# Block-sparse attention with a gated convolution: all transfers planned as one stream, four query/key pairs turned on TensorE instead of six, and the third batch's convolution done on both query parts at once

## The chip, the cores and the metric

The kernel runs on one core of one Trainium2 chip. The metric is device time in microseconds (us) of one execution. Each execution carries a state, fast or slow, and comparisons below use fast runs unless a sentence says otherwise. A ratio is the mean time of one kernel's fast runs over the mean of the other kernel's fast runs of the same rounds, so it is not quite the ratio of the medians quoted beside it; the brackets are its 95% interval.

Names: PE is TensorE (matmuls), PEld its weight loads, DVE VectorE, ACT ScalarE, POOL GpSimd, SP SyncE. A suffix q ("SPq") is an engine's instruction queue, where transfers are issued.

## The reference

Four batches, eight heads, 768 tokens, 64 columns a head. The attention mask keeps the window, the first and last blocks and three random blocks of each row of blocks. The attention output goes into a feed-forward layer with a three-tap convolution along the sequence and a sigmoid gate.

```python
scores = scale * np.matmul(q, k.transpose(0, 1, 3, 2))
scores = np.where(mask, scores, -1000000000.0)       # mask: per block of 32 x 32
attn = np.exp(scores - max); attn /= attn.sum(-1)    # shortened
x = (attn @ v) as (batch, seq, 512)                  # shortened
h = np.maximum(x @ w_in, 0.0)                        # 512 -> 1024
conv_out[s] = sum over k of conv_w[k] * h[s + k - 1] # shortened
out = (h * sigmoid(conv_out)) @ w_out                # 1024 -> 512
```

## The kernel before

The program is planned before it is built. Every piece of work is an operation with a duration per engine, dependences and buffers. A list scheduler places the operations one after the other in a model of the engines, some passes back and forth, and what comes out is a fixed order of instructions for each engine. On the chip each engine keeps its order; an instruction whose input is not there holds up everything behind it (below, VectorE stands 7.41 us before a copy, and the copy behind it, whose own input was there, starts only after it). The durations and latencies of the model therefore change the order and hardly the work (a few operations, relus and output copies, may go to VectorE or ScalarE, as the planner finds). The two latencies of DMA transposes:

```python
XLAT, TLAT = 3.908, 9.2201     # comment added here: XLAT for attention results, TLAT for a pair's q and k, in us
```

The heads are worked on in 16 pairs. A pair's q and k must be transposed into the tiles `et` and `ot` of one of the slots. The first `NPE` pairs are turned by TensorE and evicted from PSUM; the rest go through a DMA transpose into `tmp`, and VectorE copies `tmp` to the slot:

```python
NSLOT = 6
NPE = 6
...
t0 = op({"SP": 1.3}, xp(0), due - 8, [lq], alloc=tb, uses=[nb], lat=TLAT)     # transpose of q
t1 = op({"SP": 1.3}, xp(1), due - 8, [lk], uses=[nb, tb], lat=TLAT)           # transpose of k
ce = op({"DVE": 0.5}, put(ET, 0), due, [t0, t1, slot_first.get(P - 1)], alloc=slot_b[P], uses=[tb])
co = op({"DVE": 0.5}, put(OT, 64), due, [ce], uses=[slot_b[P], tb])
```

A batch has two query parts of 384 tokens, each with 18 exponentials of 128x1024, 144 in all. The convolution works on 2 x 384 columns at a time (three multiplies, two additions, a tanh, "+1", a product with h):

```python
m1 = op({"DVE": tm}, mul(1, 0), due + 1.7, list(relus) + [cw_op], alloc=cb, uses=[heb])
m0 = op({"DVE": tm}, mul(0, 1), due + 2, [edge[0]], uses=[cb, heb])
ad1 = op({"DVE": t_d2(768)}, add, due + 2.2, [m1, m0], uses=[cb])
...
th = op({"ACT": 0.745}, ...Tanh...)
```

The mask is 24 extra rows of `et` and `ot`, the same in every slot. They are built once in slot 0 and copied; from slot 2 on SyncE copies them by DMA (`rows_to`), for slot 1 VectorE and GpSimd do.

The softmax here doesn't subtract the row's maximum and nothing guards it: scores larger than these inputs give would overflow.

## Time and profile before

| | before |
|---|---|
| median of the runs | 215.1 us (214.3 to 215.75) |
| profiled span | 214.9 us |
| first exponential starts / last ends | 8.2 / 184.5 us |
| VectorE busy / idle | 189.7 / 25.2 us |
| copies of `tmp` to a slot | pairs 6 to 15; VectorE never waits for one |

In this kernel VectorE's copies of a DMA-transposed tile find it there every time: among its waits there is none for `tmp`. The view of the tile `tmp` (line, engine, operation, count, duration ns min/median/max, first and last start; then the time from issue to landing):

```profile
L581 SPq DMA_TRANSPOSE tmp<-nat x20: 1211/1365/2948, 38.8 to 128.1; - x20
L424 DVE COPY et<-tmp x10: 542/544/741, 57.4 to 145.0; 64x1536 bf16<-64x1536 bf16 x10
DMA to landing us min/median/max: 6.0/6.5/6.9
```

The transposes begin at 38.8 us. The trace has the landing of only four of the twenty; these took 6.0 to 6.9 us, under the allowance of 9.2. The engines' busy lines and the stages are shown in the prediction below. Because busy and idle of VectorE add up to the span, I use those two numbers for every kernel later: a change in work shows in the first, a change in waiting in the second.

### The profile page before, as it was taken

Reading aid. Unit: us, or ns where it says so; the run is one execution under the profiler, and the core shown is the slowest. Engines: PE = TensorE matmul, PEld = TensorE weight load, DVE = VectorE, ACT = ScalarE, POOL = GpSimd, SP = SyncE. Lnnn points to the kernel's source line nnn. Section 1 sums busy time; section 2 is a strip of 40 time slices with the busy share of each in tenths; the row PEclk is TensorE's granted clock in tenths of the full one; section 3 lists DMA queues with packets and bytes.
Section 4 is the critical chain, followed back from the end, with each engine's and each line's share of the span. In section 5 each row is a group of like instructions: output and inputs, shape, how many; then the busy total and the mean of one; then the engine's idle time right before and its main releaser. Section 6 shows DMA issues by size and latency. Waiting matters only on the chain.

```text
span 214.9 us, 6588 instructions
## 1 busy us (share of the span) xinstructions
PE 198.8 (92%) x2579; PEld 150.4 (70%) x2596; DVE 189.7 (88%) x541; ACT 182.1 (85%) x227; POOL 81.8 (38%) x174
## 2 busy tenths in 40 slices
PE   7996999997999979999989999989999999998992
PEld 4785878886677857788768667667786787554441
DVE  6865627999989999479999999999999999999972
ACT  4595999999989989999998799989999999674541
POOL 8993414625505540446375302431241012443300
PEclk9999999999999999999999999999999999999999
DMA  6999994999999997899996993001110230022223
GB/s 170 152 177 204 199 203 61 142 154 134 190 136 212 150 119 80 148 146 213 168 136 106 129 204 107 18 20 62 59 23 21 71 116 21 18 98 101 99 98 146
DMA packets 50520, 25.84 MB, mean 120 GB/s; under 512 B 36321, under 2 KB 47353, under 8 KB 50489
## 3 DMA queue, kind: packets, MB, share of 16 engines
q0 software_dynamic: 18464, 11.14, 43.7%
q1 hardware_dynamic: 31592, 13.75, 31.6%
q10 hardware_dynamic: 432, 0.52, 0.7%
q8 instruction: 20, 0.33, 0.6%
q14 instruction: 12, 0.09, 0.2%
HBM read 23.08 MB, written 6.29 MB: 137 GB/s over the span
## 4 chain that ended last, share of the span: by engine, by line
DVE 59%; PE 15%; DMA 10%; ACT 6%; issue 5%; POOL 2%; SPq 1%; ACTq 0%; DVEq 0%; POOLq 0%
DVE m L753 19%; DVE m L759 10%; DVE hE L742 7%; PE st L678 6%; ACT pt L685 5%; DVE gT L781 5%; DVE xtok L631 5%; DMA nat<-in_k_dram 4%; DMA tmp<-nat 4%; PE mix L799 4%; DVE tn L772 3%; PE av L705 2%; DMA o2s<-in_q_dram 2%; DVE o2s L424 2%; PE st L799 2%
## 5 line engine op out<-in xcount | busy, mean ns | idle before, releaser
L685 ACT ACTIVATE pt<-st 128x1024 bf16<-128x1024 f32 x144 | 141.8, 1039 | 8.5 <-PE st L678 7.2
L705 PE MATMUL av<-vt,pt 128*128 128x65 bf16 x1152 | 57.9, 193 | 1.9 <-DVE vt L519 1.4
L753 DVE TENSOR_SCALAR m<-hE,cw 128x384 bf16<-128x384 bf16 x192 | 56.9, 346 | 0.2
L705 PEld LDWEIGHTS <-pt 128*128 128x128 bf16 x1152 | 50.4, 97 | 6.2 <-issue 1.7
L729 PE MATMUL mix<-xT,winb 128*128 128x384 bf16 x240 | 48.1, 325 | 1.9 <-DVE hE L742 1.1
L829 POOL COPY hE<-hE 128x254 bf16<-128x254 bf16 x32 | 18.4, 575 | 74.7 <-DVE hE L742 51.0
L799 PE MATMUL mix<-woutb,gT 128*128 128x512 bf16 x151 | 41.0, 379 | 2.4 <-DVE gT L781 1.6
L678 PE MATMUL st<-ot 88*128 88x128 bf16 (+1 forms) x224 | 42.5, 234 | 0.5 <-ACT pt L685 0.2
L678 PE MATMUL st<-et,ot 88*128 88x128 bf16 (+1 forms) x224 | 42.5, 234 | 0.1
L678 PE MATMUL st<-et 88*128 88x128 bf16 (+1 forms) x208 | 40.7, 239 | 1.7 <-ACT pt L685 1.7
L678 PEld LDWEIGHTS <-ot 88*128 88x128 bf16 x448 | 34.5, 97 | 10.1 <-issue 0.9
L678 PE MATMUL st<-ot,et 88*128 88x128 bf16 (+1 forms) x208 | 40.7, 239 | 0.7 <-ACT pt L685 0.4
L678 PEld LDWEIGHTS <-et 88*128 88x128 bf16 x416 | 32.3, 97 | 9.9 <-issue 3.3
L759 DVE TENSOR_TENSOR m<-m 128x768 bf16<-128x768 bf16 x64 | 35.1, 554 | 0.1
L769 ACT ACTIVATE tn<-m 128x768 bf16<-128x768 bf16 x32 | 27.7, 866 | 5.5 <-DVE m L759 5.4
L729 PEld LDWEIGHTS <-winb 128*128 128x128 bf16 x256 | 22.1, 97 | 13.1 <-issue 2.7
L799 PEld LDWEIGHTS <-gT 128*128 128x128 bf16 x200 | 16.5, 98 | 15.5 <-DVE gT L781 3.1
L742 DVE TENSOR_SCALAR hE<-mix 128x384 bf16<-128x384 f32 x37 | 20.2, 548 | 3.9 <-PE mix L729 3.8
L781 DVE TENSOR_TENSOR gT<-tn,hE 128x768 bf16<-128x768 bf16 x32 | 17.9, 562 | 0.1
L631 DVE TENSOR_TENSOR xtok<-av,rcp 128x384 bf16<-128x384 f32 x32 | 17.6, 549 | 0.3
L492 POOL DMA_DIRECT2D vn<-in_v_dram x16 | 11.9, 743 | 10.4 <-DVE vt L519 8.7
L830 POOL COPY hE<-hE 128x254 bf16<-128x254 bf16 x32 | 15.3, 479 | 0.0
(76 smaller groups left out, 168.7 us busy)
## 6 DMA issues: line engine op xcount, KB each, us to landing
out_dram<-o2s SPq DMA_DIRECT2D x23, 256.0 KB, 2.2
vn<-in_v_dram POOLq DMA_DIRECT2D x16, 192.0 KB, 6.2
nat<-in_q_dram POOLq DMA_DIRECT2D x15, 192.0 KB, 7.3
nat<-in_k_dram POOLq DMA_DIRECT2D x15, 192.0 KB, 6.4
winb<-in_moe_w_in_dram POOLq DMA_DIRECT2D x2, 512.0 KB, 12.2
woutb<-in_moe_w_out_dram POOLq DMA_DIRECT2D x2, 512.0 KB, 9.5
xT<-xtok SPq DMA_TRANSPOSE x27, 8.8
o2s<-in_k_dram ACTq DMA_DIRECT2D x2, 192.0 KB
```

What stands on the lines that cost most here:

```text
L631: nm = op({"DVE": 0.475}, lambda e: nc.vector.tensor_tensor(out=xtok_t[xk.index].rearrange("p c h d -> p h c d"), in0=o_of()[:, :, :, 0:64 ...
L678: nc.tensor.matmul(out=st_t[stb.index][:, 128 * x:128 * (x + n_)], lhsT=QK[kc % 2][s][0:88, 1, hh, kc // 2, :], rhs=QK[par][s][0:88, 0, hh ...
L685: e_op = op({"ACT": t_act(1024)}, lambda e, stb=stb, ptb=ptb: nc.scalar.activation(out=pt_t[ptb.index], in_=st_t[stb.index], func=AF.Exp, ...
L705: nc.tensor.matmul(out=av_t[av_buf[(n, P % 4)].index][:, off:off + 65], lhsT=pt_t[ptb.index][:, 128 * x:128 * x + 128], rhs=VT[P % NSLOT][ ...
L729: nc.tensor.matmul(out=tiles[hb.index][:, 0:384], lhsT=winb[:, fc, 128 * ffc:128 * ffc + 128], rhs=xT_t[xt_buf[n].index][:, fc, :], start= ...
L742: nc.vector.tensor_scalar(out=dst, in0=src, scalar1=0.5, scalar2=0.0, op0=ALU.mult, op1=ALU.max)
L753: nc.vector.tensor_scalar(out=m_t[cb.index][:, slot, o0:o1], in0=src, scalar1=w, scalar2=None, op0=ALU.mult)
L759: nc.vector.tensor_tensor(out=m[:, 0], in0=m[:, 0], in1=m[:, 1], op=ALU.add)
L769: th = op({"ACT": 0.745}, lambda e: nc.scalar.activation(out=tn_t[cb.index], in_=m_t[cb.index][:, 0], func=AF.Tanh, bias=0.0, scale=0.5), ...
L781: nc.vector.tensor_tensor(out=o, in0=t, in1=h, op=ALU.mult)
L799: nc.tensor.matmul(out=acc()[:, 0:o1 - o0], lhsT=gT_t[gb.index][:, ffc, 128 * c:128 * c + 128], rhs=woutb[:, ffc, o0:o1], start=(ffc == 0) ...
L829: nc.gpsimd.tensor_copy(out=h[:, f0:f0 + 2, 1:128], in_=h[:, f0:f0 + 2, 384:511])
```

## The change

The intent is to lighten all three compute engines and the early stream of loads at once: the planner models all transfers as one stream and issues loads a fixed time ahead; mask rows are copied by VectorE instead of DMA; two pairs fewer use TensorE and PSUM; the third batch's convolution works on both query parts in one instruction.

```diff
-FLEX = 0.0345
+FLEX = 0
+PATIENCE = {"PE": 0.1, "ACT": 0, "DVE": 0.05}
...
-                    k = (s, o.prio, o.key)
+                    k = (max(s, t + PATIENCE.get(e, 0.0)), o.prio, o.key)
...
-    NSLOT = 6
-    NPE = 6
+    NSLOT = 5
+    WIDE = (2,)
+    AHEAD = 11.181113366977723
+    NPE = 4
...
-    NTMP, NVN, NNAT, NPT, NXK, NXT, NHE, NCV, NGT, NOS = 2, 3, 3, 5, 3, 4, 3, 3, 4, 4
+    NTMP, NVN, NNAT, NPT, NXK, NXT, NHE, NCV, NGT, NOS = 2, 3, 3, 5, 3, 4, 2, 2, 2, 4
-    m_t = many(NCV, [128, 2, 768], BF16, "m")
-    tn_t = many(NCV, [128, 768], BF16, "tn")
+    m_t = many(NCV, [128, 2, 1536], BF16, "m")
...
-    XLAT, TLAT = 3.908, 9.2201
+    XLAT, TLAT = 1.0, 1.1986797974651535
...
+    def sp_dma(fn, sp, dur, prio, deps, lat, alloc=None, uses=(), by="SP"):
+        i_ = op({by: sp}, fn, prio, deps, lat=0.1, alloc=alloc, uses=uses)
+        return op({"DQ": dur}, None, prio, [i_], lat=lat, uses=list(uses) + ([alloc] if alloc else []))
...
-                m[s] = op({"SP": 0.46}, rows_to(t[s], t[0]), T(4.5 * s) - 6, [m[0]], lat=6.0, ...
+                m[s] = op({"DVE": 0.58}, rows_by(t[s], t[0]), T(4.5 * s) - 2.5, [m[0]])
...
-            t0 = op({"SP": 1.3}, xp(0), due - 8, [lq], alloc=tb, uses=[nb], lat=TLAT)
+            t0 = sp_dma(xp(0), 1.25, 1.1, due - 8, [lq], TLAT, alloc=tb, uses=[nb])
...
-        ad1 = op({"DVE": t_d2(768)}, add, due + 2.2, [m1, m0], uses=[cb])
+        ad1 = op({"DVE": t_d2(w)}, add, due + 2.2, [m1, m0], uses=[cb])      # w = 1536 in the wide batch
```

Cut: the new layout of `hE` and `gT` with both query parts in one tile, the edge columns, the tail, and the other knobs of the plan.

## The prediction

The 0.13, 0.07 and 0.11 us saved for each instruction that goes were estimates; what the traces show of them stands below the text.

> **What bounds the kernel now.** I read the page first (busy shares, the 40 slices, the chain), then a table of busy time by stage, then ScalarE's, VectorE's and SyncE's instructions in order of time, and last the groups with their shapes.
>
> ```profile
> PE 198.8 (92%) x2579; PEld 150.4 (70%) x2596; DVE 189.7 (88%) x541; ACT 182.1 (85%) x227; POOL 81.8 (38%) x174
> PE   7996999997999979999989999989999999998992
> DVE  6865627999989999479999999999999999999972
> ACT  4595999999989989999998799989999999674541
> DVE 59%; PE 15%; DMA 10%; ACT 6%; issue 5%; POOL 2%; SPq 1%; ACTq 0%; DVEq 0%; POOLq 0%
> ```
>
> No single engine is the bound. All three compute engines are over 85% busy, each with a hole at another place: VectorE early, ScalarE at the end. The chain is VectorE for 59%, and most of that lies after 36 us. I cut the span where the pictures change: the first exponential (8.2), the end of ScalarE's early gaps (21.2), VectorE becoming full (36), the last exponential ending (184.5), and the last copies (209.9). Columns are the window, its length, then busy us and count of PE, PEld, DVE, ACT and POOL, the clock, DMA share and GB/s.
>
> ```profile
> 0.00:8.20 8.20, 6.91 (x47) 4.57 (x48) 5.74 (x31) 3.23 (x7) 7.34 (x16) 1.00 0.84 161
> 8.20:21.20 13.00, 10.42 (x169) 9.14 (x167) 8.77 (x19) 9.90 (x11) 9.08 (x12) 1.00 1.20 184
> 21.20:36.00 14.80, 14.20 (x238) 12.29 (x235) 8.10 (x22) 14.35 (x15) 4.99 (x10) 1.00 1.14 168
> 36.00:184.50 148.50, 142.03 (x2001) 111.86 (x2013) 142.37 (x401) 140.65 (x171) 52.82 (x120) 1.00 0.79 113
> 184.50:209.90 25.40, 24.02 (x129) 11.82 (x130) 23.58 (x70) 13.65 (x25) 7.56 (x18) 1.00 0.22 84
> ```
>
> So there are four problems in a row. In 8.2 to 21.2, 10 exponentials of some 0.91 us take 13 us: ScalarE loses about 4 us here and DMA is full. In 21.2 to 36 ScalarE is full, VectorE only 8.1 of 14.8. In the long stage PE, DVE and ACT each leave only 6 to 8 of 148.5 us: a gain needs all three lighter. The end is VectorE's (23.6 of 25.4), the convolution of the last batch.
>
> The early loss has names. These are ScalarE's exponentials and SyncE's copies of the mask rows, in order of time (start, length, operation, count, idle time and its end).
>
> ```profile
> 12.86 3.94 ACT L685 ACTIVATE pt<-st 128x1024 bf16<-128x1024 f32 x4 [0.41 <-PE st L678]
> 17.96 1.02 ACT L685 ACTIVATE pt<-st 128x1024 bf16<-128x1024 f32 x1 [1.17 <-PE st L678]
> 21.16 9.72 ACT L685 ACTIVATE pt<-st 128x1024 bf16<-128x1024 f32 x10 [0.99 <-PE st L678]
> 7.55 0.87 SPq L445 DMA_DIRECT2D et<-et  x1
> 11.53 0.71 SPq L445 DMA_DIRECT2D ot<-ot  x1
> ```
>
> The chain, in order of time, has at that place one long transfer (start, length):
>
> ```profile
> 11.27 8.96 DMA nat<-in_k_dram
> ```
>
> The gap before 21.16 is TensorE standing at the transposes of the fourth pair, whose K, issued at 11.27, lands 8.96 us later; the score matmuls sit behind them. The gap before 17.96 ends just after a VectorE copy that waited 1.49 us for V. Six mask-row transfers of 72 KB run among these loads.
>
> [...] six multiplies of 384 elements start 0.23 us apart (below, 145.46 to 146.84)[...]; two additions of 768 take 0.47 each[...]. [...]
>
> ```profile
> 145.46 1.45 DVE L753 TENSOR_SCALAR m<-hE,cw 128x384 bf16<-128x384 bf16 x6
> 146.84 1.01 DVE L759 TENSOR_TENSOR m<-m 128x768 bf16<-128x768 bf16 x2
> 147.77 0.18 DVE L629 RECIPROCAL rcp<-av 128x6 f32<-128x6 f32 x1
> ```
>
> [...] the K load above took 8.96 us with the mask rows among the loads, while the K load issued at 7.48 took 5.3. [...]
>
> **The change part by part.** The instruction order of the built kernel gives the counts.
>
> *Third batch in one go.* 48 multiplies of 384 become 24 of 768, 16 additions of 768 become 8 of 1536, 8 "+1" and 8 gates become 4 and 4, 8 tanh become 4. Elements are the same; only fixed parts go: 24 x 0.13 + 8 x 0.07 + 4 x 0.07 + 4 x 0.07 = 4.3 us of VectorE. ScalarE saves 4 x 0.11 = 0.4 (a tanh of 768 steps 0.749[...]). GpSimd's edge copies keep their elements.
>
> *Four pairs on TensorE instead of six.* 24 transposes less, about 0.056 us each: 1.3 us of TensorE. VectorE drops 8 evictions from PSUM (64x768, four for each of the two tiles, about 0.52 each: -4.1) and gains 4 SBUF copies of 64x1536 (0.48 each: +1.9): -2.2. Two more pairs go through DMA transposes, four more of them.
>
> *Mask rows.* All eight transfers by SyncE go; five slots instead of six, six more copies by VectorE, 24x1536, 0.5 to 0.76 each: +3.0 or a little more, all before 36 us where VectorE has about 6.7 us free in 21.2:36 alone. Six transfers of 72 KB are 0.44 MB, at the 0.2 MB/us of that stretch about 2 us of load stream returned (estimate).
>
> *The planner.* All transfers are planned as one stream, priority is no longer mere readiness, and ties between ScalarE and VectorE fall otherwise: VectorE gets 4 relus more (+1.9) and 2 output copies fewer (-1.2). One tail fix-up set goes (-0.3).
>
> VectorE's sum: -4.3 - 2.2 + 3.0 + 1.9 - 1.2 - 0.3 = -3.1. Counted up to the last normalisation it is 4.6 less, after it about 1.4 more; without the mask rows, which fall in the early slack, the long stage is 7.6 lighter. ScalarE before its last exponential: 25 tanh become 16 of 768 and 4 of 1536 (-9 x 0.75 + 4 x 1.39 = -1.2), 19 relus become 13 (-6 x 0.39 = -2.3), one small tanh less (-0.1): -3.7. TensorE, from its list, before the last scores: -3.9 (transposes -1.3, the rest moved behind); behind them +2.6.
>
> So before the last exponential three engines are lighter by 3.9, 7.6 and 3.7; the least counts: **-3.8**. The start: two gaps of 1.17 and 0.99 and one of 0.16 should go (-2.3), but the mask rows of pair 2 now stand on VectorE ahead of pair 1's evictions, about +0.9 at the gap before 12.86: **-1.4**. Waits between engines: of the roughly 6 us that each leaves in the long stage, VectorE's lightness should free a third: **-2.2**, the softest term. The tail: VectorE +1.4 at its real pace, TensorE +2.6 partly beside it: **+1.7**. Sum: 215.1 - 1.4 - 3.8 - 2.2 + 1.7 = 209.4.
>
> **Rivals.** (a) *A transfer takes the place.* Pairs 4 and 5 now need loads, two DMA transposes and a copy by about the 22nd exponential, where VectorE's order has that copy just before normalisations that free TensorE's accumulators. In the kernel before, transposes landed 6.5 us (median) after issue, far more than the plan's allowance. If VectorE stands there, attention stops: +2 to +4, hence 211 to 213. For it: DMA full to 130 us. Against: these loads now go ahead of the weights, and no mask rows are among them. (b) *TensorE is the real bound.* Its matmul spacing (0.22 for 512 columns, 0.16 for 384, 0.03 for 65) sums to about 190 us of the span; the change takes 1.3 of it. Then most of the VectorE relief is idle time and the result is 212 to 213. For it: 142 of 148.5 busy. Against: pipelined matmuls overcount, and the chain is mostly VectorE. (c) *The wide batch piles up.* Its convolution can start only when both query parts are through, so work moves into the tail: all eight tanh of the last batch stand after the last exponential, before it was seven. If VectorE idles before and then overflows, +3: 212. (d) *Everything unlocks.* If the three engines pack as tightly as VectorE does at 94 to 184 (99%), the friction term doubles or triples: 205 to 206.
>
> **Range and chances.** The three hard terms give 211.6 without the friction gain; (a), (b) or (c) alone put it at 212 to 213, (d) at 205. I take 205 to 213.5 for 8 in 10. The limit of 2% is 210.8, only 1.4 below which my number lies: faster 0.62, same 0.33, slower 0.05. Slower would need (a) and (c) together.
>
> **What would show it.** Start right: no gap near a microsecond before the 9th and 11th exponentials, K of the fourth pair landing two or more us earlier, a larger gap before the 5th. Long stage right: last exponential ending at 176 to 179, against 184.5; wrong if it ends above 181, and then a wait for a transposed tile on VectorE says (a), TensorE without idle says (b). Wide part right: multiplies of 768 stepping 0.33 us, additions of 1536 about 0.87, VectorE busy down by 3 to 5 us. Tail right: 31 to 33 us from last exponential to end, (c) if over 34.

The two traces can be asked for these savings (medians from the start of one instruction to the next, where the engine runs without a gap). A multiply takes 0.229 us for 384 elements in both kernels and 0.329 for 768 in the changed one, so a saved multiply is worth 2 x 0.229 - 0.329 = 0.13. An addition takes 0.469 for 768 and 0.869 for 1536: 0.07. A gate takes 0.468 and 0.869: 0.07. A tanh in the changed kernel takes 0.749 and 1.388: 0.11. The "+1" takes 0.268 for 768 and 0.568 for 1536, so its 4 x 0.07 is not shown; gates and "+1" together are level (below). On rival (b): a matmul of 384 columns stands in the trace for 0.326 us, and the next starts 0.162 us after it, so the busy times of matmuls overlap.

## The result, and the profile after

The changed kernel is correct and slower: 229.5 us in the median of four runs (226.4 to 231.5) against 215.1, ratio 1.0573 [1.0474, 1.0671]. Two of the four runs (230.7 and 231.5) count as slow, so the ratio rests on 226.4 and 228.3. The prediction was 209.4 with a range of 205.0 to 213.5. The profiled run, a fast one, spans 224.7 us, 9.8 more than before. (The profiled run of the kernel before took 216.6 us, 1.5 above its median; so the stages below differ by 9.8 us in all, where the means of the fast runs, 227.4 and 215.1, differ by 12.3.)

The page of the changed kernel, engines and 40 slices of 5.6 us, then the chain by engine:

```profile
PE 202.8 (90%) x2572; PEld 151.5 (67%) x2572; DVE 188.6 (84%) x503; ACT 181.5 (81%) x220; POOL 82.0 (37%) x158
PE   7999825999879999999998998989999999799992
DVE  6999503699996999838989969899999999999951
ACT  4799933699979999998989997979999899575450
PEclk9999985799999999999999999999999999999998
DVE 36%; PE 24%; DMA 19%; issue 8%; POOL 5%; ACT 3%; SPq 3%; DVEq 0%; ACTq 0%; POOLq 0%
```

VectorE and ScalarE are no busier in sum than before, so the 9.8 us are idle time of theirs. The sixth to eighth slices (28 to 45 us) show a hole in all three engines at once, which the kernel before does not have, with the granted clock (PEclk, the share of TensorE's full clock) falling behind it. And DMA's part of the chain has gone from 10% to 19%. By stage, with the columns of the prediction's table (the DMA share is the time of all packets over that of 16 engines, so it can exceed 1), and below them the stretch from 36 to 45 us of the kernel before:

```profile
8.00:21.20 13.20, 12.78 (x219) 11.54 (x217) 12.58 (x27) 12.61 (x14) 12.69 (x17) 1.00 1.28 167
21.20:36.00 14.80, 7.63 (x136) 6.62 (x133) 4.96 (x14) 8.38 (x10) 2.24 (x4) 0.88 1.31 179
36.00:45.00 9.00, 8.78 (x88) 6.94 (x88) 4.61 (x12) 5.83 (x7) 1.90 (x4) 0.63 1.26 174
45.00:190.80 145.80, 139.21 (x1945) 108.35 (x1942) 133.55 (x345) 134.65 (x155) 49.82 (x98) 1.00 0.71 103
```

```profile
36.00:45.00 9.00, 9.00 (x156) 8.01 (x154) 8.82 (x22) 8.56 (x10) 3.74 (x8) 1.00 1.12 126
```

From 21.2 to 36 ScalarE works 8.4 of 14.8 us, where before it worked 14.4. From 36 to 45 only 88 matmuls pass, where before it were 156, at a mean granted clock of 0.63. TensorE stood from 29.5 to 36.2 us. The granted clock was 1.00 from 21.2 to 29.5, 0.99 from 29.5 to 32.4, 0.50 from 32.4 to 42.5 and 1.00 from 42.5 to 60. It was still 0.50 for 6.3 us after the first matmul, from 36.2 to 42.5, with TensorE busy for 6.28 of them; what sets these times was not shown:

```profile
32.40:42.50 10.10, 6.28 (x53) 4.88 (x53) 3.23 (x8) 3.45 (x4) 2.12 (x4) 0.50 1.30 189
```

Where the span went, from the starts of the exponentials in both traces:

| stage | before, us | after, us | difference |
|---|---|---|---|
| start to 19th exponential | 28.7 | 26.1 | -2.6 |
| 19th to 28th | 9.4 | 19.0 | +9.6 |
| 28th to end of the last | 146.4 | 145.7 | -0.7 |
| end of the last to the end | 30.4 | 33.9 | +3.5 |

The stall of +9.6 us in one stretch of nine exponentials is nearly the whole loss. Here is what stands there. VectorE's instructions in order of time (start, length, engine, line, operation, count, in brackets the idle time before it and what ended it):

```profile
27.39 0.56 DVE L640 TENSOR_TENSOR xtok<-av,rcp 128x384 bf16<-128x384 f32 x1
35.35 0.55 DVE L434 COPY et<-tmp 64x1536 bf16<-64x1536 bf16 x1 [7.41 <-DMA tmp<-nat]
35.83 0.34 DVE L434 COPY xT<-mix 128x384 bf16<-128x384 bf16 x1
...
42.95 0.55 DVE L434 COPY et<-tmp 64x1536 bf16<-64x1536 bf16 x1 [1.07 <-DMA tmp<-nat]
```

TensorE's longest wait (line, what it waits for, us in total, times, longest), and ScalarE at the same place:

```profile
PE mix L743 <- DVE xT L434: 6.7, 1, 6.7
```

```profile
36.73 0.49 ACT L754 ACTIVATE hE<-mix 128x384 bf16<-128x384 f32 x1 [6.83 <-PE mix L743]
```

Read together: VectorE stands 7.4 us at the copy of pair 4, whose transpose has not landed. The next instruction in its order, the copy of `xT`, is ready (TensorE's transposes for it end at 28.34) but starts only at 35.83. TensorE stands 6.7 us at a matmul that needs that `xT`, with all further scores behind it, and ScalarE stands 6.8 us for TensorE. One late transfer empties three engines. Pair 4 itself is not used before 54.7, 19 us after the copy: nothing needed it yet.

Why the transfer was late. Some of the transfers issued from 15 to 46 us in the changed kernel (tile, queue, count, KB each, median us from issue to landing):

```profile
winb<-in_moe_w_in_dram POOLq DMA_DIRECT2D x2, 512.0 KB, 11.1
woutb<-in_moe_w_out_dram POOLq DMA_DIRECT2D x2, 512.0 KB, 17.9
tmp<-nat SPq DMA_TRANSPOSE x4, 14.0
```

The transposes of pairs 4 and 5, issued at 19.56 to 29.16, took 9.9 to 14.4 us. The plan allowed 1.25 us to issue one, 1.1 on the stream and 1.2 after it, some 3.6 in all, besides what it lets a transfer wait for the stream. A transpose issued at 49.9, with the DMA share at 0.60, landed in under 3 us, so the plan's figure is nearly right for a quiet stream; these four, with the share at 1.3, took 6 to 11 us longer. In the kernel before, none was issued that early.

The wide convolution did what it should. VectorE's groups by form (busy us, mean ns) in the changed kernel, three narrow batches against one wide:

```profile
L775 DVE TENSOR_SCALAR m<-hE,cw 128x384 bf16<-128x384 bf16 x144 | 41.6, 339 | 1.3 <-POOL hE L853 0.8
L781 DVE TENSOR_TENSOR m<-m 128x768 bf16<-128x768 bf16 x48 | 26.6, 562 | 0.2
L775 DVE TENSOR_SCALAR m<-hE,cw 128x768 bf16<-128x768 bf16 x24 | 9.9, 464 | 0.0
L781 DVE TENSOR_TENSOR m<-m 128x1536 bf16<-128x1536 bf16 x8 | 8.0, 1001 | 0.0
```

One narrow batch costs a third of 41.6 and of 26.6, so 13.9 and 8.9 us; the wide one 9.9 and 8.0. But these sums count the stretch twice in which one instruction ends while the next has begun (a multiply of 384 lasts 0.31 us in the median, and the next instruction starts 0.23 us after it). Counted from each instruction's start to the next one's, multiplies take 12.7 and 9.3 us (0.14 for each of the 24 saved), additions 7.9 and 7.4, and gates and "+1" are level: 4.0 us less, where I had 4.3.

### The profile page after: what moved, and what is told of

It reads as the page before. It is cut to its first block, busy times and chain, and to the rows that moved or that the text cites. A ratio compares the mean times of both kernels' runs of the same rounds, so it can differ in the third digit from the quotient of the medians.

```text
span 224.7 us, 6501 instructions
## 1 busy us (share of the span) xinstructions
PE 202.8 (90%) x2572; PEld 151.5 (67%) x2572; DVE 188.6 (84%) x503; ACT 181.5 (81%) x220; POOL 82.0 (37%) x158
## 3 DMA queue, kind: packets, MB, share of 16 engines
q0 software_dynamic: 18464, 11.14, 39.9%
## 4 chain that ended last, share of the span: by engine, by line
DVE 36%; PE 24%; DMA 19%; issue 8%; POOL 5%; ACT 3%; SPq 3%; DVEq 0%; ACTq 0%; POOLq 0%
DMA tmp<-nat 13%; DVE m L775 12%; PE mix L813 7%; PE st L692 7%; DVE m L781 7%; PE mix L743 4%; DVE hE L756 4%; DMA nat<-in_q_dram 4%; PE av L719 3%; DVE gT L794 3%; DVE xtok L640 3%; SPq L590 3%; POOL nat L497 2%; DVE m L792 2%; PE st L813 2%
## 5 line engine op out<-in xcount | busy, mean ns | idle before, releaser
L699 ACT ACTIVATE pt<-st 128x1024 bf16<-128x1024 f32 x144 | 139.7, 1034 | 9.6 <-PE st L692 8.3
L743 PE MATMUL mix<-xT,winb 128*128 128x384 bf16 x240 | 49.3, 329 | 8.1 <-DVE xT L434 6.7
L775 DVE TENSOR_SCALAR m<-hE,cw 128x384 bf16<-128x384 bf16 (+1 forms) x168 | 51.5, 357 | 1.3 <-POOL hE L853 0.8
L813 PE MATMUL mix<-woutb,gT 128*128 128x512 bf16 x168 | 44.1, 379 | 3.6 <-DVE gT L794 2.6
L851 POOL COPY hE<-hE 128x254 bf16<-128x254 bf16 x48 | 24.7, 542 | 58.3 <-DVE hE L756 46.1
L692 PE MATMUL st<-et,ot 88*128 88x128 bf16 (+1 forms) x224 | 42.9, 236 | 0.0
L692 PE MATMUL st<-et 88*128 88x128 bf16 (+1 forms) x208 | 41.7, 242 | 0.8 <-ACT pt L699 0.7
L781 DVE TENSOR_TENSOR m<-m 128x768 bf16<-128x768 bf16 (+1 forms) x56 | 34.6, 625 | 0.2
L790 ACT ACTIVATE m<-m 128x768 bf16<-128x768 bf16 (+1 forms) x28 | 26.5, 945 | 9.5 <-DVE m L781 9.3
L756 DVE TENSOR_SCALAR hE<-mix 128x384 bf16<-128x384 f32 x42 | 23.0, 548 | 5.8 <-PE mix L743 5.7
L434 DVE COPY et<-tmp 64x1536 bf16<-64x1536 bf16 x12 | 6.9, 578 | 15.6 <-DMA tmp<-nat 15.5
L794 DVE TENSOR_TENSOR gT<-m,hE 128x768 bf16<-128x768 bf16 (+1 forms) x28 | 17.4, 623 | 0.1
```

Of the source, the lines that this page charges most:

```text
L692: nc.tensor.matmul(out=st_t[stb.index][:, 128 * x:128 * (x + n_)], lhsT=QK[kc % 2][s][0:88, 1, hh, kc // 2, :], rhs=QK[par][s][0:88, 0, hh ...
L699: e_op = op({"ACT": t_act(1024)}, lambda e, stb=stb, ptb=ptb: nc.scalar.activation(out=pt_t[ptb.index], in_=st_t[stb.index], func=AF.Exp, ...
L743: nc.tensor.matmul(out=tiles[hb.index][:, 0:384], lhsT=winb[:, fc, 128 * ffc:128 * ffc + 128], rhs=xT_t[xt_buf[n].index][:, fc, :], start= ...
L756: nc.vector.tensor_scalar(out=dst, in0=src, scalar1=0.5, scalar2=0.0, op0=ALU.mult, op1=ALU.max)
L775: nc.vector.tensor_scalar(out=split(m_of(slot))[:, y], in0=hE_t[hb.index][:, f0 + y, sl, 128 * x:128 * x + 384], scalar1=cw[:, x, f0 + y:f ...
L781: nc.vector.tensor_tensor(out=m_of(0), in0=m_of(0), in1=m_of(1), op=ALU.add)
```

## The experiments

The theory after the first look was: **the allowance.** The plan takes transfers to land in 1.2 us; they land in 10 to 14 us; VectorE's order is therefore wrong. Rivals: the backlog of weight loads ahead of the transposes is to blame and not the plan; the wide batch; fewer pairs on TensorE; the planner's new rules whatever the work. Eighteen kernels ran, each against the kernel before on the same chip. Busy and idle of VectorE are those of the profiled run, idle being span less busy; the 28th exponential of the kernel before starts at 38.1 and its last ends at 184.5. The medians take in runs in the slow state (two each of the changed kernel and r4xw, one each of puts45_later, npe6 and tlat9_narrow); the ratios don't. Planned again, or re-planned, means that the order of the whole program is new.

| kernel | differs | median us | ratio [95%] | 28th exp. starts | last exp. ends | VectorE busy / idle |
|---|---|---|---|---|---|---|
| changed kernel | | 229.5 | 1.057 [1.047, 1.067] | 45.1 | 190.8 | 188.6 / 36.1 |
| puts45_later | order only | 228.5 | 1.059 [1.052, 1.066] | 37.2 | 196.6 | 188.8 / 41.7 |
| puts_all_later | order only | 239.9 | 1.114 [1.105, 1.123] | 37.3 | 202.9 | 190.0 / 46.8 |
| loads_later | order only | 226.8 | 1.051 [1.042, 1.059] | 45.6 | 190.9 | 189.8 / 35.0 |
| tlat9 | TLAT 9.22 | 220.3 | 1.023 [1.017, 1.028] | 36.8 | 184.9 | 190.7 / 27.7 |
| tlat9_narrow | the same, no wide batch | 223.8 | 1.040 [1.037, 1.043] | 37.2 | 188.0 | 191.3 / 30.7 |
| npe6 | NPE 6 | 227.1 | 1.056 [1.053, 1.059] | 39.9 | 198.5 | 189.8 / 43.1 |
| r4w | four pairs, wide, re-planned | 224.5 | 1.044 [1.040, 1.047] | 37.1 | 191.7 | 187.4 / 35.5 |
| r4n | four, narrow, re-planned | 220.9 | 1.028 [1.023, 1.033] | 35.1 | 185.0 | 189.1 / 29.2 |
| r6w | six, wide, re-planned | 218.1 | 1.015 [1.013, 1.018] | 40.8 | 182.7 | 191.8 / 24.7 |
| r6n | six, narrow, re-planned | 217.1 | 1.011 [1.008, 1.013] | 38.3 | 182.1 | 191.9 / 23.5 |
| r4x | four, narrow, loaded latencies | 220.6 | 1.027 [1.023, 1.031] | 37.3 | 189.6 | 190.1 / 28.8 |
| r4xw | four, wide, loaded latencies | 221.5 | 1.022 [1.013, 1.030] | 37.6 | 185.6 | 186.7 / 32.8 |
| r6m | r6n with four narrow buffers | 217.2 | 1.009 [1.007, 1.012] | 37.8 | 180.8 | 192.6 / 23.1 |
| r8m | r6m with eight pairs | 217.8 | 1.013 [1.011, 1.016] | 38.5 | 184.4 | 196.4 / 19.5 |
| before_rows_dve | before, mask rows on VectorE | 220.6 | 1.026 [1.022, 1.029] | 37.8 | 189.1 | 195.8 / 23.0 |
| before_npe4 | before, four pairs, re-planned | 218.2 | 1.010 [1.002, 1.017] | 37.9 | 187.3 | 188.5 / 27.7 |
| before_npe4_b | the same, another plan | 215.4 | 1.003 [0.993, 1.013] | 36.7 | 184.1 | 187.6 / 25.9 |
| before_npe8 | before, eight pairs, re-planned | 223.4 | 1.033 [1.026, 1.041] | 36.4 | 190.3 | 192.2 / 29.4 |

The profiles of puts45_later and npe6 are of slow runs, so their last three columns are only a rough guide. Three of the four edits of the kernel before gave a wrong result (before_rows_dve, before_npe4, before_npe8: relative error 0.32 to 0.34); the cause was not found. They do the instructions that they should and their times are reported, but with the cause unknown no conclusion rests on them alone; before_npe4_b, which is correct, carries the argument.

### Moving the copies, moving the loads

*puts45_later* and *puts_all_later* keep the changed kernel's plan and only put the copies of `tmp` later in VectorE's order, pairs 4 and 5 alone or all pairs, limited by the pair's first use and by the next user of the `tmp` buffer.

```diff
-        for o in sc.run(PASSES):
+        for o in later(sc.run(PASSES), {4: 9.0, 5: 11.5}):     # us later; all: 6.0 for the others
```

> The changed kernel with only VectorE's four copies out of the transposed tiles of pairs 4 and 5 moved later in its order (planned start +9 and +11.5 us, still ahead of their first use); loads, transposes and all other engines' orders are unchanged. Theory 1, the plan lets VectorE stand before a transfer that has not landed: the 7.4 and 1.1 us waits before these copies disappear, exponential 27 starts near 36 us instead of 45, the clock's dip at 32 to 45 us goes, and the time is 229.5 - 8 to -11 = 218 to 221. Rival, the time is lost to the wide batch or to a fuller tail and the stall only moves idle time: 227 or more.

> As before, and the copies of pairs 6 to 15 also moved up to 6 us later. Theory 1: all of VectorE's 15.5 us of waits for transposed tiles go, 213 to 218. If the later waits (3.5 us at 100, 1.0 at 115, 1.8 at 135) lay beside slack: same as with pairs 4 and 5 alone.

Both missed. The stall at 35 went, the 28th exponential started at 37.2, and another came. VectorE of puts45_later, at pair 6:

```profile
56.61 0.55 DVE L434 COPY et<-tmp 64x1536 bf16<-64x1536 bf16 x1 [6.86 <-DMA tmp<-nat]
```

There are two `tmp` buffers. A later copy frees its buffer later, the transpose of the pair after next is issued later (44.7 and 47.4), and lands at 52.3 and 56.5. With all copies moved there are four such waits, of 3.2 to 6.9 us, one of them for v. So patching the order at one place moves the wait to the next place where the plan trusts 1.2 us.

*loads_later* takes part of the backlog away: the second weight matrix and the loads of pair 6 are issued after 29 us instead of ahead of the transposes.

```diff
+        for x, o in enumerate([wts[0][0], wts[1][0]] + list(loads[6])):
+            o.start = max(o.start, 29.2 + 0.1 * x)
```

> The changed kernel's VectorE order kept, but GpSimd issues the two loads of the output weights and those of pair 6 behind planned time 29 us instead of at about 17 to 25. If the transposes of pairs 4 and 5 take 14 us because these 2.9 MB share the DMA engines with them, pair 4's second transpose lands near 29 us instead of 35.3, the wait before its copy shrinks from 7.4 to under 2.5 us, and the time falls by 5 to 8 us, to 221 to 225. If transposes are slow by themselves: landing and time as before, 227 to 231.

Mostly a miss: 226.8 us. Pair 5's transposes did speed up, from about 14 to about 8 us, but pair 4's second half landed at 36.0:

```profile
36.12 0.55 DVE L434 COPY et<-tmp 64x1536 bf16<-64x1536 bf16 x1 [6.37 <-DMA tmp<-nat]
```

The stream stayed full (DMA share 1.29 from 29 to 36 us, 1.31 in the changed kernel), with the first weight matrix, pair 5 and then the moved loads. So the backlog is not these loads alone; which share each has was not tested.

### The allowance alone

*tlat9* gives back one number and lets the planner plan again.

```diff
-    XLAT, TLAT = 1.0, 1.1986797974651535
+    XLAT, TLAT = 1.0, 9.2201
```

> The changed kernel planned again with the transposes' latency of the kernel before (9.22 us instead of 1.20), nothing else. Theory 1: waits of VectorE for transposed tiles below 3 us, 210 to 215, at or a little under the kernel before. Rival, the change's other parts are what is slow: 222 or more.

220.3 us. Between the means of the fast runs, 7 of the 12.3 us come back (227.4 to 220.4; the ratio falls from 1.057 to 1.023), with one number and no change in the program's operations. The 28th exponential starts at 36.8, earlier than before's 38.1. VectorE's waits for `tmp` (total, times, longest), first the changed kernel, then this one:

```profile
DVE et L434 <- DMA tmp<-nat: 15.5, 6, 7.4
```

```profile
DVE et L434 <- DMA tmp<-nat: 2.1, 2, 1.6
```

That is the main cause shown, as far as a plan that is new throughout can show it. The transposes of pairs 4 and 5 are as slow here (10.7 to 14.8 us); VectorE is only sent to them later. But the expectation of 210 to 215 was missed by 5 us: the kernel is still 2.3% slower than before, with a lighter long stage (VectorE 136.0 us busy from the 28th exponential to the last, before 140.3) that takes 148.1 us against 146.4.

*npe6* keeps the short allowance and gives the two pairs back to TensorE.

```diff
-    NPE = 4
+    NPE = 6
```

> The changed kernel planned again with six pairs turned by TensorE instead of four, nothing else (the optimistic 1.20 us of transfer latency stays). If the loss is that pairs 4 and 5 were moved to DMA transposes in the one stretch where the DMA engines have a backlog: the 7.4 us wait before their copies is gone, exponential 27 starts at 36 to 39 us instead of 45, later waits for transposed tiles remain, time 215 to 222. If the head is slow for another reason: 226 or more.

227.1 us, in the range that I had given to "another reason". Taking pairs 4 and 5 off the DMA transposes removes the stall at 35, and the next trusting copies stall instead:

```profile
108.84 0.55 DVE L434 COPY et<-tmp 64x1536 bf16<-64x1536 bf16 x1 [7.99 <-DMA tmp<-nat]
```

*tlat9_narrow* is tlat9 with `WIDE = ()`.

> The kernel with 9.22 us of planned transpose latency, with the third batch done in two query parts like the others. If the wide convolution costs time by piling work up (it can begin only when both parts are through): 2 to 4 us faster than 220.3. If it gains what its fixed parts say (4.3 us of VectorE, where VectorE is not alone the bound): 1 to 4 us slower, 221 to 224.

It is some 3 us slower than its wide twin, with a stall of 4.4 us of its own, before 63.4 us, where VectorE waits for TensorE. So the wide batch is not what loses; whether it gains can't be read from one pair of plans, as the next experiments showed.

*before_rows_dve* is the kernel before with one part of the change, mask rows by VectorE (result wrong).

```diff
-                m[s] = op({"SP": 0.46}, rows_to(t[s], t[0]), T(4.5 * s) - 6, [m[0]], lat=6.0, ...
+                m[s] = op({"DVE": 0.58}, rows_by(t[s], t[0]), T(4.5 * s) - 2.5, [m[0]])
```

> The kernel before with the mask rows of slots 2 to 5 copied by VectorE instead of SyncE's eight transfers, planned again, nothing else. The prediction's term for the start: the gaps before exponentials 9 and 11 shrink from 1.17 and 0.99 us to under 0.4, K of pair 3 lands two us earlier than 20.24, exponential 19 starts 1 to 2.5 us before 28.7, and the time is 213 to 215. If the rows' transfers did not hold up the loads: landing unchanged, time 215 to 217.

220.6 us. K of the fourth pair, issued at 11.0 us, landed at 16.1 and not at 20.2, so the mask rows' transfers did hold it up. Yet the 19th exponential starts at 28.2 against 28.7, a little of the hoped-for gain. The eight copies add to VectorE's work (195.8 us against 189.7), but all before 27 us. From the 28th exponential to the last, VectorE has as much to do as before (140.5 us and 140.3) and takes 151.3 us for it, not 146.4, with two waits of 2.1 and 2.8 us at 83 and 128. This was the first warning that a new plan costs something by itself: its planned length is 202.5 us, before's is 202.1. With the result wrong, it is no more than a warning.

### Two by two, with plans searched again

To compare work and not plans, I set XLAT to 3.9 and TLAT to 9.2 in the changed kernel, and searched the plan's knobs (pace, offsets, AHEAD, passes) anew for each of four variants, for the shortest planned length: four or six pairs, third batch wide or narrow.

```diff
-    XLAT, TLAT = 1.0, 1.1986797974651535
+    XLAT, TLAT = 3.9, 9.2
-    NPE = 4        # r6w, r6n
+    NPE = 6
-    WIDE = (2,)    # r4n, r6n
+    WIDE = ()
```

> Four pairs on TensorE and the wide batch as in the changed kernel, but with the latencies of the kernel before (9.2 us for a pair's transpose, 3.9 us for the results' transposes) and the plan's knobs searched again to the shortest planned span (201.6 us, which the planner gives this kernel; the changed kernel's own was 202.1). Theory A (the only thing wrong with the change is the two latencies; its lighter engines are worth what I predicted for work and friction): no stall over 2 us before the 27th exponential and 209 to 213 us, so faster than before. Theory B (the plan no longer fits the chip in small ways all along, and lighter engines alone give nothing): 217 to 221 us as the kernel with the transpose latency alone put back (220.3).

> As r4w with six pairs on TensorE (planned span 205.1). Theory A (the pairs given away are worth what I predicted, some 2 us): 211 to 216 us, 2 us above r4w. Theory B (plans of equal kind all come out alike on the chip): within 1.5 us of r4w.

> As r4w with all batches narrow (planned span 203.4). Theory A (the wide batch is worth its lighter VectorE work): 2 to 4 us above r4w, as the earlier narrow kernel was 3.5 us above its wide twin. Theory B: within 1.5 us of r4w.

> Six pairs on TensorE and all batches narrow: the work of the kernel before with the mask rows on VectorE, but in the changed kernel's planner (planned span 204.0). Theory A: near the kernel before, 214 to 217 us. Theory B (planner and shared buffers of the changed kernel cost something whatever the work is): 219 to 223 us.

Theory A, that lighter engines are worth what I predicted, falls: the lightest kernel, r4w (VectorE 187.4 us), is the slowest at 224.5, and the heaviest, r6n (191.9), the fastest at 217.1. Theory B falls as stated too: the four are not alike. In this planner six pairs beat four by 6.4 us with the wide batch and by 3.8 with narrow ones; the wide batch costs 1.0 us with six pairs and 3.6 with four. These are single plans, and plans of one work part as widely: four pairs with the wide batch came at 220.4 (tlat9), 224.3 (r4w) and, below, 219.8 us (r4xw), as means of fast runs. So the cost of the wide batch is not shown; that of four pairs in this planner holds better, as each of the six plans with four pairs and a long allowance for them (219.8 to 224.3) is slower than each of the three with six (217.2 to 218.2). TensorE's list of r4w shows where its largest wait has moved, to the other allowance:

```profile
63.51 0.48 PE L743 MATMUL mix<-xT,winb 128*128 128x384 bf16 x1 [4.33 <-DMA xT<-xtok]
```

The transposes of the attention results, for which it allows 3.9 us, took 8.6 to 11.0 us from 35 to 66 us in that run, where their landing was recorded.

### Allowances as measured under load; buffers; the opposite direction

*r4x* and *r4xw* plan the four-pair kernels with what was measured: 15 us for the transposes of pairs 4 to 7 and 11 us for the attention results of the first three query parts, 5 and 4 us later.

```diff
-            t0 = sp_dma(xp(0), 1.25, 1.1, due - 8, [lq], TLAT, alloc=tb, uses=[nb])
+            t0 = sp_dma(xp(0), 1.25, 1.1, due - 8, [lq], 15.0 if P < 8 else 5.0, alloc=tb, uses=[nb])
-        xtr[(n, hp)] = sp_dma(tr, 1.2, 0.8, due - 5, [nm], XLAT, uses=[xk] + us, alloc=al)
+        xtr[(n, hp)] = sp_dma(tr, 1.2, 0.8, due - 5, [nm], 11.0 if n < 3 else 4.0, uses=[xk] + us, alloc=al)
```

> Four pairs on TensorE, narrow, planned with the latencies that were measured under load (15 us for the transposes of pairs 4 to 7, 11 us for the first three result transposes, 5 and 4 us later); knobs searched again (planned span 208.8). Theory D1 (the loss of the four-pair kernels lies in the plan's allowance alone): no wait over 1.5 us for a transposed tile, and at or below the six-pair kernel's 217.1, 213 to 217. Theory D2 (the load itself costs: two more pairs through an already full stream can only be waited for, wherever the plan puts the wait): 219 to 223, like the 220.9 of its twin with 9.2 us.

> The same with the wide third batch (planned span 208.7): the changed kernel with honest latencies. D1: 212 to 217. D2: 220 to 225, like the 224.5 of its twin.

r4x took 220.6 us, as D2 said. The fast runs of r4xw took 218.3 and 221.3, one under D2's range and one in it, both over D1's; its ratio of 1.022 counts as unclear. The waits for `tmp` are gone from r4x and down to one of 2.6 us in r4xw; what VectorE waits for now is TensorE. In r4xw:

```profile
DVE rcp L638 <- PE av L719: 7.0, 3, 2.8
```

So honest allowances remove the named wait. What remains over the six-pair kernels (r4x 3.4 us over r6m, the fast runs of r4xw 1.6 over r6w) shows no one large wait; VectorE's longest for TensorE are 4.4 us in r4x and 3.0 in r4xw.

*r6m* tests the tail: four convolution buffers of 768 columns in place of two of 1536, the same memory. *r8m* puts eight pairs on TensorE.

```diff
-    NTMP, ..., NHE, NCV, NGT, NOS = 2, ..., 2, 2, 2, 4
+    NTMP, ..., NHE, NCV, NGT, NOS = 2, ..., 2, 4, 2, 4
-    m_t = many(NCV, [128, 2, 1536], BF16, "m")
+    m_t = many(NCV, [128, 2, 768], BF16, "m")
```

> Six pairs on TensorE, narrow, with four buffers of the convolution of 768 columns in place of two of 1536 (the same memory), searched again (planned span 203.0). Theory T1 (the tail of 33 us after the last exponential, against 30.4 before, comes from the shared pair of convolution buffers): tail 30 to 31.5 and 214 to 215.5. Theory T2 (the tail is only work left over by the plan): tail 32.5 to 34 and 216.5 to 218.

> As r6m with eight pairs on TensorE (planned span 203.7), the direction opposite to the change. If load of the stream before 60 us is what decides, pairs 6 and 7 off it bring 1 to 2 us more than r6m (213.5 to 215.5); if VectorE's evictions (+2.2 us) or TensorE decide once the stream is no longer late, it is 1 to 3 us slower than r6m (217 to 219).

r6m: 217.2 us, level with r6n, so T1 falls for the convolution buffers; the shared tiles of `hE` and `gT` were not tested. Its last exponential ends 3.7 us earlier than before's, and its tail is longer by more than that. The window from the last exponential to the end, of before, then of r6m (columns as above):

```profile
184.50:214.90 30.40, 25.21 (x137) 12.49 (x137) 24.70 (x72) 14.02 (x26) 7.56 (x18) 0.99 0.25 96
```

```profile
180.80:215.70 34.90, 28.99 (x156) 14.52 (x157) 28.63 (x87) 17.17 (x32) 9.69 (x24) 1.00 0.26 94
```

VectorE does 28.6 us of work there instead of 24.7, and TensorE 29.0 instead of 25.2. An earlier last exponential gains nothing if the convolutions behind it were only put off. The changed kernel's tail reads alike: 27.0 us of VectorE in 33.9. r8m is at 217.8, with VectorE 3.8 us busier than r6m and 3.6 us less idle: more evictions, fewer waits, no net gain. The opposite direction does not beat the kernel before either.

### The disputed part alone, in the planner of before

All this said that two pairs moved to the stream lose. The test of it is the kernel before with this part alone, its own planner and allowances, knobs searched anew; twice with different plans, and once with eight pairs.

```diff
-    NPE = 6
+    NPE = 4        # before_npe8: 8
```

> The kernel before with one part of the change alone: four pairs on TensorE in place of six, its own planner, its own allowances, the knobs of the plan searched anew (planned span 201.7; the kernel before has 202.1). Theory P (moving two pairs onto the full stream is what loses, in any planner): 218 to 222 us, 3 to 7 over before. Theory Q (it loses only in the changed planner): 213 to 216.

> The same kernel with another plan from another search (planned span 202.0), to see how far two plans of equal planned length part on the chip: theory P 218 to 222, Q 213 to 216; a difference of over 3 us between the two plans would say that plan scatter is as large as the effects told apart here.

> The kernel before with eight pairs on TensorE, knobs searched anew (planned span 201.5). Theory P with a stream still late at six pairs: 213 to 215. If six already freed the stream in time, VectorE's added evictions (2.2 us by the prediction's figures) show: 216 to 218. Theory Q: 214 to 217, no order.

before_npe4_b is at 215.4, ratio 1.003 [0.993, 1.013]: no loss, or one of 1.3% at most. So theory P (218 to 222 in any planner), and with it the reading that the load on the stream must cost, falls with this one correct plan. Its twin before_npe4 came at 218.2, at the edge of P's range, but with a wrong result. The stream is as full there as in the slow four-pair kernels. The window from 30 to 60 us, of before_npe4_b, then of r4x (columns as above; the number before the last is the DMA share):

```profile
30.00:60.00 30.00, 28.09 (x385) 21.69 (x384) 25.94 (x71) 28.34 (x35) 12.98 (x28) 1.00 1.40 171
```

```profile
30.00:60.00 30.00, 26.05 (x388) 21.09 (x390) 23.52 (x65) 27.37 (x32) 13.54 (x24) 1.00 1.35 185
```

The transposes are as slow too, as far as their landing is recorded (three of the first eight: 9.0, 16.6 and 5.9 us), yet VectorE waits for none: the copies of pairs 4 and 5 start at 42.9 and 48.0, 4.7 and 4.2 us before the pairs' first exponentials (in the changed kernel 19 and 16 us before). The page's first line of before_npe4_b:

```profile
PE 199.1 (93%) x2553; PEld 150.2 (70%) x2572; DVE 187.6 (88%) x538; ACT 182.0 (85%) x226; POOL 81.2 (38%) x174
```

VectorE has 2.1 us less to do than before (the prediction had 2.2 for this part) and idles 0.7 us more. The profiled span is 213.5 us; those of the kernel before in the same rounds are 212.7 to 215.2, so that is no gain.

The twin plan before_npe4, whose planned length is within 0.4 us, has a ratio of 1.010 [1.002, 1.017]. The two intervals overlap, so this pair doesn't show how far equal plans part. The better measure is the four-pair kernels with the wide batch above: three plans of one work, all correct, from 219.8 to 224.3 us, a scatter of 4.5 us or 2%. It is as large as several of the differences between re-planned kernels above, and it limits what they can say. before_npe8 missed every expectation (223.4), with one wait of 4.4 us for a transposed tile at 126 us: again one bad place in a plan, not the work.

## Why the prediction was wrong

By its own steps:

- **Start, -1.4: right, and better.** The 19th exponential starts 2.6 us earlier. The gaps before the 9th and 11th are gone; the feared +0.9 before the 5th did not come, the first nine run without a gap. K of the fourth pair landed at 15.5 instead of 20.2, and before_rows_dve, if with a wrong result, says that the mask rows had held it up.
- **Rival (a), a transfer takes the place: this is the step that failed.** The prediction named the very copy and the consequence ("If VectorE stands there, attention stops: +2 to +4"), saw that the allowance was far below the 6.5 us of the kernel before, sized it at +2 to +4, and left it out of the sum. The stretch with the stall measured +9.6. Two things made it larger than sized. The 6.5 us was the median of four recorded landings, none issued before 52 us; on the full early stream it is 10 to 14 us. And the copy was not near its use: it stood 19 us ahead of it, in front of an `xT` copy that everything needed, so the full lateness became a stop of three engines, with TensorE at half clock until 42.5. The argument against, "these loads now go ahead of the weights", held for pair 4's loads (issued at 13.9 and 14.6) and was untrue for the transposes: both weight matrices were issued from 15.3 to 19.8 us, all but the last half ahead of pair 4's first transpose at 19.6.
- **Work, -3.8, and friction, -2.2: not realised.** From the 28th exponential to the last the kernel takes 0.7 us less, not 6. The work did shrink: VectorE does 133.6 us there, and the wide batch saved 4.0 us. It came back as idle time. Part of that is rival (a) once more: four further waits for transposed tiles, 7.0 us in all, from 94 to 135 us. But tlat9, almost without such waits, doesn't gain there either. A gain of this kind needs a plan that fits the chip as well as the old one; I had taken for granted that the new one would.
- **Tail, +1.7: right in sign, too small.** It measured +3.5, mostly VectorE work left behind the last exponential (27.0 us against 24.7). Not the convolution buffers: r6m.
- **Wide part: right.** Multiplies of 768 start 0.33 us apart in the median and additions of 1536 0.87, as foretold. Only VectorE's busy sum fell by 1.1, not 3 to 5. Mask rows and relus are no excuse, as the prediction's -3.1 had them. Counted from start to start, each term came near its size: convolution -3.8 (foretold -4.3), pairs -1.9 (-2.2), mask rows +2.9 (+3.0), relus +2.0 (+1.9), output copies -1.1 (-1.2). The rest, some +0.7, is spread over small instructions.
- **Slips in the sum.** The wide batch's parts make 4.24, not 4.3; ScalarE's 3.6, not 3.7; and the least of 3.9, 7.6 and 3.7 is not 3.8. Each is 0.1 us at most.
- **Rivals (b), (c), (d).** (d) is out. (b), TensorE as bound, is not what made the stall: TensorE stood idle in it. (c) holds for part of the tail at most, as narrow kernels have the long tail too.

What is shown: the stall, its chain through three engines, and that some 7 us of the 12 come back with the allowance alone. What is shown against the further story, by one correct plan: fewer pairs on TensorE need not lose, nor need the load on the stream. What stays open: which of the other parts, the planner's patience, its stream model, five slots, or mask rows on VectorE, keeps the remaining 1 to 4% in the re-planned kernels; against a scatter of 2% between plans of the same work, these runs can't tell. No version here beats the kernel before.

## What to carry to other kernels

In a statically ordered program a latency allowance is part of the kernel: take it from landing times in the stage where the transfer is issued, under that stage's load, and place the copy close to its use, not at the first moment that the model thinks it possible, but not so late either that its buffer holds up the next transfer (puts_all_later). An instruction that waits costs what stands behind it in its engine's order (here 7.4 us on VectorE, then 6.7 on TensorE and 6.8 on ScalarE), so size such a risk by the whole lateness and by who waits next, and put it into the sum. And before believing that less work gives less time, ask whether the new order is as good as the old one; compare a change with two plans of each kind, since plans of the same work parted by 2% here.
